# Attention sums and a three-way maxout layer on one core: transposing the normalised k and v sums on VectorE instead of TensorE

## The chip, the cores and the metric

The kernel runs on one NeuronCore of a Trainium2 chip. A core has five engines that run side by side, each with its own queue of instructions in order: TensorE (PE in the profile; its weight loads are shown as PEld), VectorE (DVE), ScalarE (ACT), GpSimd (POOL) and SyncE (SP). TensorE reads SBUF and writes PSUM, which here is eight banks of 2 KB on each of 128 partitions. The metric is the device time of one execution in microseconds (us), as the median of several runs.

## The reference

Two parts in a row. The first one squeezes k and v of each of 8 batches and 8 heads (576 positions, 64 wide) to 32 slots, and lets q attend to the slots; the second one takes the largest of three linear maps of the result, and maps that back:

```
a = exp(phi - max(phi)) ; a = a / sum(a over positions)      # phi: 8, 8, 576, 32
k_m = einsum('bhsm,bhsd->bhmd', a, k) ; v_m = einsum('bhsm,bhsd->bhmd', a, v)
attn = softmax(q @ k_m^T / 8) ; x = attn @ v_m               # per batch and head
x -> (8 * 576, 512)
h = max(x @ w1, x @ w2, x @ w3)                              # w: 512 x 768
out = h @ w_out                                              # 768 x 512
```

## The kernel before

The work goes batch by batch, but the batches overlap. Heads are taken in pairs: NP = 4 pairs, NG = 2 halves, and slots of four pairs fill 128 partitions (M = 32 slots each). The maps w1 and w2 have w3 subtracted once, so that x @ w3 is added only at the end; and the weights are multiplied into the slots of v ("fold"), so that x itself is never formed.

For each batch these steps run; the letter is the one that the order uses for it:

- L0 to L3 load phi, k, v and q through GpSimd's queue (lines 94, 98 and 111), which casts k, v and q to bf16; r0 and r1 pack k and v into one tile kvr on GpSimd (line 104). Tiles of two buffers each are loaded again as soon as their readers are done; a load that waits for them holds up GpSimd's queue behind it.
- E is the exponential of phi on ScalarE (line 258). B sums k, v and ones over the positions with 72 small matmuls into PSUM (line 278).
- N normalises on VectorE: a reciprocal (298), v times it (302), and k times it in two instructions (312). They fill kvn, 128 partitions by three blocks of 128 (v, and k as even and odd columns).
- K transposes the three blocks of kvn, 128 x 128 each, by three matmuls against the identity (line 327) into one PSUM bank, and one copy brings the result to kvt (128 x 384, bf16; line 189 on ScalarE or 193 on VectorE). Batches 0 and 1 do k and v apart, as K0 and K1.
- Q0 and Q1 transpose q on VectorE (342). S multiplies k's part of kvt with q (362), 32 small matmuls, and takes the exponential (371).
- a, s, c, m, X turn the scores to attention for batches 1 to 7: transpose in blocks of 32 (416), sum (424), reciprocal (433) on VectorE, multiply on GpSimd (438), transpose back (446) on VectorE. Batch 0 does it in another way (M, R).
- D0 to D2 and D3 fold v's part of kvt into the weights (matmuls of line 469, evacuated to wp or wp3). D4 and V belong to batch 0 alone.
- F0 to F11 are the hidden layer (495): four matmuls each. The even one is evacuated as h (187 on ScalarE, 191 on VectorE), the odd one is combined with it by a maximum on VectorE (508).
- T0 to T4 are the last layer: six matmuls of line 557 with the hidden values and two of line 542 with the slots (four of line 533 for T4), an evacuation to ot and a store on SyncE's queue. P does three of the six ahead, p the two with the slots.

Nothing is scheduled automatically: a long string at line 652 lists the steps, and each engine executes its share of them in that order. "!" after a step swaps the engine of its evacuation between ScalarE and VectorE, "^" splits the evacuation in two halves, one for each. A second string of digits (line 146) names the PSUM bank of each step that needs one. So a step that stands behind another in the string waits for it on every engine that both use. The part around the change, in the order before:

```
L1@4 a1@2 L2@4 T2@1! s1@2 ... E@3 F2@2 F3@2 L2@5 L1@5 F8@2 F0@2 F9@2 B@3 N@3 D3@2 F1@2
P3@2 Q0@3 L0@5 Q1@3 F4@2 P2@2 K@3! p2@2 F5@2 S@3 ...
```

Of the kernel before, what the change touches and what calls it, by code (L numbers as in the profile page):

```python
# [9 lines left out]
BF16 = mybir.dt.bfloat16  # L10
# [5 lines left out]
def kernel(  # L16
# [12 lines left out]
    nc = tc.nc  # L29

    B, H, S, D = q.shape
    M = phi.shape[-1]
    P = 128
    NP = H // 2
    NG = NP // 2
    HP = P // 2
    NC = S // HP
    R = 32
# [3 lines left out]
    SH = S // 2  # L42
    BANK = 512
    HEAD = 3

    const = ctx.enter_context(tc.tile_pool(name="const", bufs=1))
    inp = ctx.enter_context(tc.tile_pool(name="inp", bufs=2))
    work = ctx.enter_context(tc.tile_pool(name="work", bufs=2))
# [74 lines left out]
    def load_wo():  # L123
        nc.gpsimd.dma_start(out=wo_sb, in_=moe_w_out.rearrange("(t p) c -> p t c", p=P))
# [16 lines left out]
    for i in range(P // M):  # L141
# [4 lines left out]
    banks = iter(  # L146
        "".join(
            """
            60606026024506014014024062406420461246246742404462642602462046246367404603260260
            42062046274240402606206420462406142142646204764260426046206426402762604260420624  # L150
            07042604506421026264124026420402462064206026462467676767
            """.split()
        )
    )
# [1 line left out]
    def one_bank():  # L156
        return psum[:, int(next(banks))]
# [50 lines left out]
    def w3_o_head(j):  # L208
        po = one_bank()
        for f in range(HEAD):  # L210
            nc.tensor.matmul(
# [5 lines left out]
            )  # L217
        w3_heads[j] = po, HEAD

# [28 lines left out]
        )  # L248

    ln = const.tile([P, S], FP32, name="ln")  # L250
    ONES = {(0, 0), (0, 1)}
    st = {}

# [37 lines left out]
    def att_kv_norm(b, part=None):  # L291

        s = st[b]
        kvp = s["kvp", part]
        if part != 1:
            rden = s["rden"] = work.tile([P, NG], FP32, name="rden")
            s["kvn"] = work.tile([P, 3, P], BF16, name="kvn")
            nc.vector.reciprocal(out=rden, in_=kvp[:, :, D if part == 0 else 2 * D])
        rden, kvn = s["rden"], s["kvn"]
        if part != 0:  # L300
            v0 = 0 if part == 1 else D
            nc.vector.tensor_tensor(
                out=kvn[:, 0].rearrange("p (a d) -> p a d", a=NG),
                in0=kvp[:, :, v0 : v0 + D],
                in1=rden.unsqueeze(2).to_broadcast([P, NG, D]),
                op=ALU.mult,
            )
        if part == 1:
            return
        for g in range(NG):  # L310
            kn = kvn[:, 1:3, HP * g : HP * (g + 1)]
            nc.vector.tensor_scalar_mul(
                out=kn.rearrange("p h (t d) -> p h t d", t=2),
                in0=kvp[:, g, 0:D]
                .rearrange("p (d h) -> p h d", h=2)
                .unsqueeze(2)
                .to_broadcast([P, 2, 2, R]),
                scalar1=rden[:, g : g + 1],
            )

    def att_kv_t(b, swap, part=None):

        s = st[b]
        ns = {None: slice(0, 3), 0: slice(1, 3), 1: slice(0, 1)}[part]
        ps = one_bank().bitcast(BF16)[:, 0 : 3 * P].rearrange("p (n m) -> p n m", n=3)
        for n in range(3)[ns]:
            nc.tensor.transpose(ps[:, n], s["kvn"][:, n], ident)  # L327
        if part != 1:
            s["kvt"] = work.tile([P, 3, P], BF16, name="kvt")
        evacuate("K", 0, swap, s["kvt"][:, ns], ps[:, ns])  # L330
        if b == 0 and part != 0:
            s["kvtn"] = const.tile([P, P], BF16, name="kvtn")
            nc.scalar.mul(out=s["kvtn"], in_=ps[:, 0], mul=-1.0)

    def att_q(b, n):


        s = st.setdefault(b, {})
        if "qT" not in s:
            s["qT"] = work.tile([P, NP, NC, R, 2], BF16, name="qT")  # L340
        j = halves[n]
        nc.vector.transpose(  # L342
            out=s["qT"][:, j].rearrange("p j c r e -> p (j c r e)").bitcast(FP32),
            in_=loaded[b]["q"][:, j].rearrange("p j c d -> p (j c d)").bitcast(FP32),
        )
# [270 lines left out]
    def issue(b, n, swap):  # L616

        i = int(n[1:]) if len(n) > 1 else None
        {
            "I": lambda: [make_identity(nc, ident)]  # L620
            + [nc.gpsimd.memset(x[:, :, :, 2 * D : 2 * D + 1], 1.0) for x in kvrs],
            "Y": lambda: load_w(i) if i < 3 else load_wo(),
            "L": lambda: load_ph(b) if i == 0 else load_q(b) if i == 3 else load_kv(b, i - 1),
            "H": lambda: load_kv(b, i % 2, halves[i // 2]),
            "r": lambda: pack(b, i),
            "E": lambda: [att_exp(b, h) for h in (halves if b == 0 else [slice(0, NP)])],
            "B": lambda: att_kv(b, i),
            "N": lambda: att_kv_norm(b, i),
            "K": lambda: att_kv_t(b, swap, i),
            "Q": lambda: att_q(b, i),  # L630
            "S": lambda: att_score(b),
            "a": lambda: att_t(b, i),
            "s": lambda: att_sum(b, i),
            "c": lambda: att_rec(b, i),
            "m": lambda: att_mul(b, i),
            "X": lambda: (ones_mul if (b, i) in ONES else att_back)(b, i),
            "M": lambda: ones_sum(b, i),
            "R": lambda: ones_rec(b, i),
            "D": lambda: fold(b, i, swap),
            "F": lambda: ffn1(b, i, swap),  # L640
            "P": lambda: ffn2_hidden(b, i, range(HEAD)),
            "p": lambda: ffn2_slots(b, i),
            "J": lambda: w3_o_head(i),
            "T": lambda: ffn2(b, i, swap),
            "W": lambda: w3_t(i, swap),
            "O": lambda: w3_o(i, swap),
            "V": lambda: w_diff(i),
            "G": lambda: wait_for(b, i),
            "Z": lambda: warm_up(i),
        }[n[0]]()  # L650


    for w in """
        E@0 H0@0 H2@0 L3@0 Z25@0 B0@0 I@0 N0@0 Z2@0 K0@0! Q0@0 Q1@0 Z9@0 S@0 Z2@0 M0@0 M1@0
        R0@0 Y2@0 G0@0 R1@0 W0@0 Y3@0 W1@0 W2@0 H1@0 H3@0 Y0@0 Z6@0 O0@0! X1@0 X0@0 Y1@0 L0@1
        O1@0 B1@0 N1@0 O3@0! L1@1 K1@0! O2@0! D1@0^ D0@0^ L3@1 D3@0^ V0@0 L2@1 F8@0 F10@0 F2@0!
        V1@0 F0@0 F6@0 L2@2 F4@0! L1@2 D2@0 V2@0 D4@0 p1@0 E@1 F3@0 F1@0 p0@0 F11@0 F5@0 F9@0
        P1@0 F7@0 B0@1 P3@0 N0@1 P0@0 Q1@1 Q0@1 K0@1! L0@2 L3@2 T1@0 L0@3 S@1 T3@0 B1@1 V4@0
        L1@3 p2@0 a0@1 s0@1 N1@1 K1@1! P2@0 c0@1 m0@1 a1@1 s1@1 c1@1 D0@1 D2@1!^ m1@1 X0@1 X1@1
        D1@1!^ T2@0 T0@0! F2@1 F6@1! F8@1 F3@1 F7@1 F0@1 L2@3 F4@1 r1@2 r0@2 F1@1 E@2 F9@1 F5@1  # L660
        F10@1 L3@3 F11@1 L0@4 P2@1 B@2 N@2 Q0@2 D3@1 T0@1! K@2! Q1@2 T1@1 S@2 a0@2 s0@2 c0@2
        L1@4 a1@2 L2@4 T2@1! s1@2 m0@2 c1@2 X0@2 D2@2 m1@2 D0@2! D1@2! X1@2 T4@1 r0@3 T3@1 r1@3
        F6@2 F10@2!^ F7@2 L3@4 F11@2 E@3 F2@2 F3@2 L2@5 L1@5 F8@2 F0@2 F9@2 B@3 N@3 D3@2 F1@2
        P3@2 Q0@3 L0@5 Q1@3 F4@2 P2@2 K@3! p2@2 F5@2 S@3 p3@2 a0@3 a1@3 s0@3 L3@5 c0@3 s1@3
        m0@3 T3@2 D0@3 D2@3!^ E@4 c1@3 X0@3 m1@3 D1@3! T2@2 T0@2! X1@3 r1@4 T1@2! F2@3 F4@3!
        r0@4 F3@3 F0@3!^ L2@6 Q1@4 F6@3 F5@3 F8@3 F7@3 F10@3 B@4 N@4 D3@3 P0@3 Q0@4 F11@3 K@4!
        F9@3 F1@3 p1@3 L1@6 L0@6 P1@3 L3@6 r1@5 D1@4! S@4 a0@4 r0@5 s0@4 c0@4 E@5 T0@3! a1@4
        T3@3 m0@4 s1@4 T1@3 c1@4 X0@4 D2@4!^ B@5 D0@4 N@5 m1@4 D3@4 Q0@5 L1@7 T4@3! X1@4 Q1@5
        K@5! F6@4!^ F8@4!^ S@5 F7@4 F9@4 F10@4 F4@4 F5@4 F0@4 F2@4 a1@5 r1@6 F11@4 L2@7 a0@5
        r0@6 F3@4 E@6 L0@7 F1@4 s0@5 T2@3! D2@5^ c0@5 D0@5 B@6 L3@7 N@6 D1@5! T1@4 s1@5 m0@5  # L670
        Q1@6 c1@5 K@6! Q0@6 m1@5 r1@7 T3@4 X0@5 X1@5 S@6 F2@5!^ a0@6 F10@5!^ F3@5 F8@5 F11@5
        F0@5 s0@6 F6@5 E@7 F4@5^ F1@5 F9@5 F7@5 a1@6 T2@4! F5@5 r0@7 D0@6^ D1@6! B@7 N@7 D3@5!^
        T0@4 Q0@7 c0@6 K@7 T2@5! D2@6!^ s1@6 c1@6 Q1@7 m0@6 D1@7 D3@7 T0@5! P3@5 S@7 a0@7 s0@7
        m1@6 a1@7 X0@6 T3@5 D2@7!^ D3@6 D0@7 X1@6 s1@7 c0@7 T4@5! F4@6 F0@6 F10@6! F8@6!^ F5@6
        c1@7 m0@7 F6@6 m1@7 F1@6 F9@6 T1@5 X1@7 X0@7 F11@6 F2@6 F10@7! F6@7 F2@7 F3@6 F7@6
        F4@7! F0@7 F11@7 T2@6 F3@7 F1@7 F7@7 T0@6 F8@7 F9@7 F5@7 T1@6! T0@7! T4@7! T1@7 T3@6
        T2@7 T3@7
    """.split():
        n, b = w.rstrip("!^").split("@")
        issue(int(b), n, w[len(n) + 1 + len(b) :])  # L680
# [30 lines left out]
```

## Time and profile before

| | before |
|---|---|
| median of 3 runs | 164.09 us (163.59 to 164.92) |
| the profiled execution | 163.59 us |
| its span, first to last instruction | 161.8 us |
| TensorE matmuls busy | 152.2 us, 2058 instructions |
| VectorE busy | 110.1 us, 212 instructions |
| ScalarE busy | 87.5 us, 140 instructions |
| GpSimd busy | 69.6 us, 72 instructions |
| granted TensorE clock | 0.995 of full speed on average |

The busy time of an engine is the time in which at least one of its instructions runs. TensorE's matmuls are pipelined, so that each lasts longer than the distance to the next. The profile also has the chain of waits: it begins at the last instruction and goes back, at each step to what released it, or to the instruction before it on its engine. Groups of instructions have the line of kernel.py that issued them (L327 is line 327), the engine, the operation, what is written and read, shapes as partitions x elements, the count, then busy time in us and the mean of one in ns.

### The profile page before, as it was taken

How to read it: one execution, taken by the hardware profiler on the slowest of the kernel's cores; microseconds unless marked ns; L12 is line 12 of the kernel's file. 1: busy time of each engine (PE TensorE's matmuls, PEld its weight loads, DVE VectorE, ACT ScalarE, POOL GpSimd, SP SyncE). 2: the span in 40 equal slices, each digit the busy share in tenths (PEclk: the TensorE clock that was granted, in tenths of full speed). 3: DMA queues.
4: the chain of work that ended last, by engine and by line, in shares of the span. 5: the costliest groups of instructions: out<-in, count | busy, mean ns of one | idle time of the engine just before them, and what ended most of it. 6: DMA issues, size and time to landing. Idle time of an engine off the chain costs nothing.

```text
span 161.8 us, 4860 instructions
## 1 busy us (share of the span) xinstructions
PE 152.2 (94%) x2058; PEld 86.0 (53%) x2080; DVE 110.1 (68%) x212; ACT 87.5 (54%) x140; POOL 69.6 (43%) x72
## 2 busy tenths in 40 slices
PE   7988799999999999999999999999999999999990
PEld 2343454664476436644764467557543477663460
DVE  2013456999997578879895988979888976774020
ACT  4104414934676595759465987768537955111310
POOL 7266224111599039915958986537204050000000
PEclk9999999999999999999999999999999999999998
DMA  5999999999999999999999999999222311013333
GB/s 151 157 200 205 201 211 209 280 208 210 233 310 296 251 239 283 301 217 208 249 311 245 209 321 282 208 289 274 69 86 95 127 65 65 0 69 124 136 130 132
DMA packets 21974, 31.77 MB, mean 196 GB/s; under 512 B 1216, under 2 KB 16576, under 8 KB 21952
## 3 DMA queue, kind: packets, MB, share of 16 engines
q0 software_dynamic: 16080, 21.43, 69.1%
q1 hardware_dynamic: 5728, 9.90, 17.5%
q8 instruction: 16, 0.26, 0.6%
q10 hardware_dynamic: 144, 0.13, 0.2%
q14 instruction: 6, 0.05, 0.1%
HBM read 39.32 MB, written 9.44 MB: 301 GB/s over the span
## 4 chain that ended last, share of the span: by engine, by line
PE 73%; DMA 14%; DVE 5%; POOL 3%; issue 2%; ACT 1%; POOLq 0%
PE psum L495 28%; PE psum L557 25%; DMA w_sb<-in_moe_w_dram 9%; PE psum L542 7%; PE psum L469 5%; DMA kvo<-in_k_dram 4%; PE psum L278 3%; DVE hT L508 2%; PE psum L362 2%; POOL t L438 1%; POOL kvo L98 1%; PE psum L533 1%; PE psum L593 1%; DVE qT L342 1%; PE psum L327 1%
## 5 line engine op out<-in xcount | busy, mean ns | idle before, releaser
L557 PE MATMUL psum<-wo_sb,hT 128*128 128x512 bf16 x194 | 50.3, 380 | 1.5 <-issue 0.9
L495 PE MATMUL psum<-attn,wp 128*128 128x288 bf16 x384 | 50.6, 286 | 0.1
L495 PEld LDWEIGHTS <-wp 128*128 128x128 bf16 x384 | 37.1, 98 | 13.2 <-issue 0.9
L508 DVE TENSOR_TENSOR hT<-psum,h 128x576 bf16<-128x576 f32 x48 | 34.4, 750 | 6.5 <-PE psum L495 3.8
L187 ACT ACTIVATE h<-psum 128x576 bf16<-128x576 f32 (+1 forms) x41 | 23.6, 609 | 14.1 <-PE psum L495 13.8
L557 PEld LDWEIGHTS <-hT 128*128 128x128 bf16 x210 | 19.0, 98 | 22.8 <-issue 4.6
L438 POOL TENSOR_TENSOR t<-t,sm 128x576 bf16<-128x576 bf16 x14 | 16.2, 1154 | 31.8 <-DVE sm L433 31.7
L189 ACT CAST wp<-psum 128x1024 bf16<-128x1024 f32 (+2 forms) x31 | 24.3, 835 | 7.4 <-PE psum L469 7.2
L104 POOL COPY kvr<-kvo 128x2304 bf16<-128x2304 bf16 x12 | 25.1, 2111 | 5.0 <-DMA kvo<-in_v_dram 2.7
L189 ACT COPY ot<-psum 128x512 f32<-128x512 f32 x26 | 15.2, 592 | 21.1 <-PE psum L542 17.5
L542 PE MATMUL psum<-wp,attn 128*128 128x512 bf16 x59 | 17.8, 379 | 0.3 <-issue 0.3
L167 PE MATMUL psum<-warm 128*128 128x512 bf16 x42 | 12.6, 457 | 1.4 <-DVE warm L136 1.2
L193 DVE COPY ot<-psum 128x512 f32<-128x512 f32 x9 | 6.1, 681 | 10.8 <-PE psum L542 10.8
L342 DVE STREAM_TRANSPOSE qT<-qq 128x576 f32<-128x576 f32 x16 | 11.8, 754 | 1.3 <-DMA qq<-in_q_dram 1.2
L371 ACT ACTIVATE e<-psum 128x576 bf16<-128x576 f32 x16 | 9.6, 651 | 4.0 <-PE psum L362 3.8
L258 ACT ACTIVATE e<-ph 128x1152 bf16<-128x1152 f32 (+1 forms) x9 | 9.6, 1061 | 2.8 <-DMA ph<-in_phi_dram 2.7
L189 ACT COPY kvt<-psum 128x384 bf16<-128x384 bf16 (+2 forms) x9 | 3.7, 410 | 13.3 <-PE psum L327 13.2
L191 DVE TENSOR_SCALAR h<-psum 128x288 bf16<-128x288 f32 (+1 forms) x15 | 8.7, 590 | 2.9 <-PE psum L495 2.9
L193 DVE CAST wp<-psum 128x512 bf16<-128x512 f32 (+2 forms) x14 | 10.1, 731 | 0.8 <-PE psum L469 0.7
L424 DVE TENSOR_REDUCE sm<-t 128x18 f32<-128x576 bf16 x14 | 10.3, 739 | 0.2
L416 DVE STREAM_TRANSPOSE t<-e 128x288 f32<-128x288 f32 x14 | 6.5, 462 | 5.8 <-ACT e L371 5.7
L111 POOL DMA_DIRECT2D qq<-in_q_dram x8 | 6.0, 756 | 9.2 <-DVE h L191 3.3
(60 smaller groups left out, 130.1 us busy)
## 6 DMA issues: line engine op xcount, KB each, us to landing
out_dram<-ot SPq DMA_DIRECT2D x35, 256.0 KB, 5.5
qq<-in_q_dram POOLq DMA_DIRECT2D x8, 576.0 KB, 16.9
ph<-in_phi_dram POOLq DMA_DIRECT2D x7, 576.0 KB, 18.7
kvo<-in_k_dram POOLq DMA_DIRECT2D x7, 576.0 KB, 19.7
kvo<-in_v_dram POOLq DMA_DIRECT2D x7, 576.0 KB, 17.1
w_sb<-in_moe_w_dram POOLq DMA_DIRECT2D x3, 768.0 KB, 14.7
wo_sb<-in_moe_w_out_dram POOLq DMA_DIRECT2D x1, 768.0 KB, 10.3
ph<-in_phi_dram SPq DMA_DIRECT2D x2, 288.0 KB, 3.2
```

The lines of the kernel that those rows point to most:

```text
L104: nc.gpsimd.tensor_copy(out=kvrs[b % 2][:, :, :, D * i : D * (i + 1)], in_=kvos[b % 2][:, 1 - i])
L167: nc.tensor.matmul(po[:, 0:BANK], lhsT=warm[:, 0:P], rhs=warm, start=True, stop=True)
L187: nc.scalar.activation(out=out_, in_=in_, func=AF.Relu)
L189: nc.scalar.copy(out=out_, in_=in_)
L193: nc.vector.tensor_copy(out=out_, in_=in_)
L342: nc.vector.transpose(out=s["qT"][:, j].rearrange("p j c r e -> p (j c r e)").bitcast(FP32), in_=loaded[b]["q"][:, j].rearrange("p j c d - ...
L424: nc.vector.tensor_reduce(out=sm, in_=s["t", g].rearrange("p n r e -> p n e r"), op=ALU.add, axis=mybir.AxisListType.X,)
L438: nc.gpsimd.tensor_tensor(out=t, in0=t, in1=s["sm", g].unsqueeze(2).to_broadcast([P, S // HP, R, 2]), op=ALU.mult,)
L495: nc.tensor.matmul(acc[:, h, 0:SH], lhsT=wps[b][:, g, w * DF + ft * P : w * DF + (ft + 1) * P], rhs=attn[:, g, c0 : c0 + SH], start=(g == ...
L508: nc.vector.tensor_tensor(out=hT[:, ft, (b % 2) * S : (b % 2 + 1) * S].rearrange("p (h n) -> p h n", h=2), in0=a, in1=s["h1", ft], op=ALU.max,
L542: nc.tensor.matmul(po, lhsT=attn[:, g, c0 : c0 + P], rhs=wp3s[b][:, g, :], start=(g == 0 and not done), stop=(last and g == NG - 1),)
L557: nc.tensor.matmul(po, lhsT=hT[:, fc, c0 : c0 + P], rhs=wo_sb[:, fc, :], start=(n == ns[0] and not done), stop=(last and n == ns[-1]),)
```

## The change

For batches 2 to 7, K is replaced by k. N writes kvn in another arrangement of columns: four groups of 96, each with 32 columns of v and of the two halves of k. Then VectorE transposes the whole kvn at once (128 x 384), in blocks of 32 x 32, into a new tile kvm. Sixteen copies put the 32-partition pieces of kvm in their places in kvt: four groups of columns times four groups of partitions, those with odd j on ScalarE, the others on GpSimd, 32 partitions x 96 elements each, to other partitions than they come from. TensorE and PSUM take no part in it. Batches 0 and 1 keep K0 and K1. The whole order is new, and with it the string of banks and the marks for the evacuations; among others, the load of phi for batch 1 comes behind that of its k, and the parts of T that are done ahead differ: P2@1 is gone, and p3@1, p1@1, p3@4 and P1@6 are new.

```diff
+    MOVED = range(2, B)
...
+    kvm = const.tile([P, P // R, 3, R], BF16, name="kvm")
...
+        if b in MOVED:
+            kb = kvn.rearrange("p n m -> p (n m)").rearrange("p (x n d) -> p x n d", x=P // R, n=3)
+            vn = kb[:, :, 0].rearrange("p (a h) d -> p a h d", a=NG)
+            kns = [kb[:, 2 * g : 2 * g + 2, 1:3].rearrange("p t h d -> p h t d") for g in range(NG)]
+        else:
+            vn = kvn[:, 0].rearrange("p (a h d) -> p a h d", a=NG, h=2)
+            kns = [
+                kvn[:, 1:3, HP * g : HP * (g + 1)].rearrange("p h (t d) -> p h t d", t=2)
+                for g in range(NG)
+            ]
...
+    def att_kv_move(b):
+
+        s = st[b]
+        nc.vector.transpose(
+            out=kvm.rearrange("p x n m -> p (x n m)"),
+            in_=s["kvn"].rearrange("p n m -> p (n m)"),
+        )
+        kvt = s["kvt"] = work.tile([P, 3, P], BF16, name="kvt")
+        for x in range(P // R):
+            for j in range(NP):
+                r = slice(M * j, M * (j + 1))
+                move = nc.scalar.copy if j % 2 else nc.gpsimd.tensor_copy
+                move(out=kvt[R * x : R * (x + 1), :, r], in_=kvm[r, x])
...
+            "k": lambda: att_kv_move(b),
...
+        R0@0 Y2@0 G0@0 R1@0 W0@0 Y3@0 W1@0 W2@0 H1@0 H3@0 Y0@0 Z6@0 O0@0! X1@0 X0@0 Y1@0 O1@0
+        L1@1 B1@0 N1@0 L0@1 O2@0! L3@1 K1@0! L2@1 O3@0! D1@0^ D0@0^ D3@0^ F10@0 F8@0 V0@0 F4@0!
+        V1@0 F0@0 F6@0 L2@2 F2@0! D2@0 V2@0 D4@0 L1@2 p1@0 L0@2 F3@0 F1@0 F11@0 p0@0 F5@0 F7@0
+        P0@0 E@1 F9@0 B0@1 N0@1 P3@0 L3@2 P1@0 K0@1! Q1@1 T1@0 Q0@1 V4@0 S@1 a0@1 s0@1 T3@0
+        B1@1 p2@0 N1@1 c0@1 L2@3 m0@1 a1@1 s1@1 c1@1 K1@1! X0@1 P2@0 D0@1 D2@1 D1@1!^ m1@1 L0@3
+        X1@1 r1@2 T0@0! T2@0 F2@1^ L1@3 F6@1! r0@2 F4@1 F0@1 F7@1 F10@1 E@2 L3@3 F5@1 F1@1 L1@4
+        F11@1 F3@1 F8@1 F9@1 B@2 D3@1 L2@4 N@2 L0@4 k@2 T0@1 p3@1 Q0@2 Q1@2 p1@1 T2@1! S@2 a0@2
+        s0@2 a1@2 c0@2 r1@3 T3@1 T1@1 m0@2 s1@2 c1@2 D2@2^ m1@2 X0@2 D1@2! D0@2^ T4@1! X1@2
+        F10@2 r0@3 F11@2 E@3 F2@2!^ F3@2 F0@2 F1@2 L3@4 F4@2 L2@5 B@3 D3@2 F6@2 N@3 k@3 Q0@3
+        F5@2 L1@5 F8@2 p2@2 F7@2 Q1@3 P3@2 P2@2 F9@2 p3@2 S@3 a0@3 T3@2 s0@3 T0@2! r0@4 T2@2!
+        a1@3 c0@3 s1@3 c1@3 L0@5 D0@3 m0@3 X0@3 m1@3 D1@3! X1@3 D2@3 T1@2! F0@3!^ F6@3!^ F1@3
+        E@4 F2@3 Q1@4 L3@5 L1@6 F7@3 F10@3 r1@4 L2@6 B@4 N@4 D3@3 F4@3 Q0@4 F8@3 k@4 F11@3 F9@3
+        F3@3 P1@3 F5@3 P0@3 p1@3 D2@4 S@4 a0@4 T1@3 T0@3! r1@5 E@5 a1@4 s0@4 s1@4 c1@4 L0@6
+        T3@3 r0@5 D1@4^ D3@4 B@5 c0@4 L3@6 m1@4 N@5 X1@4 m0@4 D0@4 k@5 Q0@5 X0@4 T4@3 Q1@5 T2@3
+        F0@4!^ r0@6 L1@7 F10@4!^ S@5 F11@4 F1@4 F2@4 a0@5 s0@5 F4@4 F8@4 F3@4 r1@6 F9@4 F6@4
...
+        D0@5 D2@5 T1@4 X1@5 Q1@6 F4@5! F0@5!^ F6@5!^ F8@5 F10@5 k@6 Q0@6 F11@5 F2@5! F1@5 F9@5
+        T2@4 S@6 a0@6 F3@5 r0@7 F5@5 F7@5 E@7 T0@4 D1@6^ r1@7 D3@5 B@7 N@7 D3@6 a1@6 k@7 Q1@7
+        Q0@7 s1@6 c1@6 P3@5 T1@5! m1@6 T2@5! s0@6 S@7 T3@5 a0@7 s0@7 D1@7! c0@6 D2@6!^ a1@7
```

More of the change, by code (lines that the diff above doesn't have):

```diff
@@ L148 @@
             """
-            60606026024506014014024062406420461246246742404462642602462046246367404603260260
-            42062046274240402606206420462406142142646204764260426046206426402762604260420624
-            07042604506421026264124026420402462064206026462467676767
+            60606026024506014014024062406420462146246742404462462042602460246745206025024062
+            46024602126424261426420642064206126460426106240624064206404602462402406246024604
+            62045026206506246024604206402604260246024110101012
             """.split()
@@ L302, in att_kv_norm @@
             nc.vector.tensor_tensor(
-                out=kvn[:, 0].rearrange("p (a d) -> p a d", a=NG),
-                in0=kvp[:, :, v0 : v0 + D],
-                in1=rden.unsqueeze(2).to_broadcast([P, NG, D]),
+                out=vn,
+                in0=kvp[:, :, v0 : v0 + D].rearrange("p a (h d) -> p a h d", h=2),
+                in1=rden.unsqueeze(2).unsqueeze(3).to_broadcast([P, NG, 2, R]),
                 op=ALU.mult,
@@ L310, in att_kv_norm @@
         for g in range(NG):
-            kn = kvn[:, 1:3, HP * g : HP * (g + 1)]
             nc.vector.tensor_scalar_mul(
-                out=kn.rearrange("p h (t d) -> p h t d", t=2),
+                out=kns[g],
                 in0=kvp[:, g, 0:D]
@@ L654 @@
         E@0 H0@0 H2@0 L3@0 Z25@0 B0@0 I@0 N0@0 Z2@0 K0@0! Q0@0 Q1@0 Z9@0 S@0 Z2@0 M0@0 M1@0
[L655 to L677, printed above, removed]
+        R0@0 Y2@0 G0@0 R1@0 W0@0 Y3@0 W1@0 W2@0 H1@0 H3@0 Y0@0 Z6@0 O0@0! X1@0 X0@0 Y1@0 O1@0
@@ new lines @@
+        T3@3 r0@5 D1@4^ D3@4 B@5 c0@4 L3@6 m1@4 N@5 X1@4 m0@4 D0@4 k@5 Q0@5 X0@4 T4@3 Q1@5 T2@3
+        F0@4!^ r0@6 L1@7 F10@4!^ S@5 F11@4 F1@4 F2@4 a0@5 s0@5 F4@4 F8@4 F3@4 r1@6 F9@4 F6@4
+        c0@5 F5@4 F7@4 p3@4 L2@7 a1@5 s1@5 m0@5 E@6 c1@5 m1@5 L0@7 L3@7 T3@4 D1@5^ B@6 X0@5 N@6
+        D0@5 D2@5 T1@4 X1@5 Q1@6 F4@5! F0@5!^ F6@5!^ F8@5 F10@5 k@6 Q0@6 F11@5 F2@5! F1@5 F9@5
+        T2@4 S@6 a0@6 F3@5 r0@7 F5@5 F7@5 E@7 T0@4 D1@6^ r1@7 D3@5 B@7 N@7 D3@6 a1@6 k@7 Q1@7
+        Q0@7 s1@6 c1@6 P3@5 T1@5! m1@6 T2@5! s0@6 S@7 T3@5 a0@7 s0@7 D1@7! c0@6 D2@6!^ a1@7
@@ L678 @@
+        D0@6^ m0@6 X1@6 T0@5 D3@7 s1@7 c0@7 c1@7 D0@7 m0@7 X0@6 D2@7 m1@7 X0@7 T4@5! F6@6 F0@6^
+        X1@7 F7@6 F2@6 F1@6 F10@6 F8@6! F11@6 F0@7 F3@6 F9@6 F10@7 F1@7 F11@7 F4@6!^ F2@7! F4@7
+        F6@7 F8@7 F5@7 F7@7 F9@7 P1@6 F5@6 F3@7 T3@6 T1@6 T4@7 T1@7! T0@6 T2@6 T0@7 T2@7 T3@7
     """.split():
```

## The prediction

> **What bounds the kernel now.** I read the chain of waits in order of time first, then the busy times, then stretches of the middle, then the single forms of instructions. The chain ends like this (start, length, what):
>
> ```profile
> 44.52 0.02 issue
> 44.55 0.49 DVE attn L446
> 45.04 0.04 issue
> 45.08 5.79 PE psum L495 x46
> ...
> 53.88 0.43 PE psum L542 x2
> 54.31 0.17 PE psum L327 x3
> 54.48 1.29 PE psum L557 x6
> ...
> 157.93 0.23 PE psum L601 x2
> 158.16 0.02 issue
> 158.19 0.37 ACT ot L613
> ```
>
> Behind 45.08 us every piece up to 158.16 is TensorE work or a few hundredths of "issue". I added those "issue" pieces up from the whole chain: 1.5 us of 113.1 us. So TensorE alone sets the time there, and work taken off it is worth its own length, as long as nothing else comes late. The three transposes of a batch (L327) stand on the chain with 0.17 us, six times for batches 2 to 7 (at 54.31, 70.02, 84.31, 94.41, 106.01 and 119.29 us). Before 45 us the chain is on the loads of the weights up to 26.4 us, then mostly on VectorE from 31.8 to 45 us; batches 0 and 1 are at work there.
>
> The stretch from 44 to 148 us, cut into seven, sums to this (busy us):
>
> ```profile
> 90.00:106.00 16.00, 15.65 (x306) 9.53 (x307) 14.34 (x32) 13.22 (x22) 11.01 (x10) 1.00 1.17 255
> ...
> sum 104.00, PE 102.44 PEld 60.93 DVE 83.72 ACT 66.75 POOL 52.55; mean PE 14.63 PEld 8.70 DVE 11.96 ACT 9.54 POOL 7.51
> ```
>
> The columns are TensorE's matmuls, its weight loads, VectorE, ScalarE and GpSimd; the granted clock is 1.00. VectorE is the next engine, 80% busy, and 90% in the fullest stretch. The forms that price the change (busy us, mean ns behind the count):
>
> ```profile
> L104 POOL COPY kvr<-kvo 128x2304 bf16<-128x2304 bf16 x12 | 25.1, 2111 | 5.0 <-DMA kvo<-in_v_dram 2.7 <-DMA kvo<-in_k_dram 2.3
> ...
> L342 DVE STREAM_TRANSPOSE qT<-qq 128x576 f32<-128x576 f32 x16 | 11.8, 754 | 1.3 <-DMA qq<-in_q_dram 1.2
> ...
> L258 ACT ACTIVATE e<-ph 128x1152 bf16<-128x1152 f32 x7 | 8.2, 1170 | 0.5 <-DMA ph<-in_phi_dram 0.5
> ...
> L416 DVE STREAM_TRANSPOSE t<-e 128x288 f32<-128x288 f32 x14 | 6.5, 462 | 5.8 <-ACT e L371 5.7
> ...
> L401 ACT ACTIVATE r<-ln 128x576 f32<-128x576 f32 x2 | 1.4, 682 | 0.1
> ...
> L621 POOL MEMSET kvr<- 128x36 bf16 x2 | 0.4, 298 | 0.0
> ...
> L131 POOL COPY gate<-kvo 1x2 bf16<-1x2 bf16 x1 | 0.2, 175 | 4.3 <-DMA kvo<-in_k_dram 4.3
> ```
>
> **What is removed.** 18 TensorE transposes: six pieces of 0.17 us on the chain, 1.02 us. Each is issued 57 ns after the one before; the 219 ns that a row gives for one is its pipelined length. Five ScalarE copies of kvt (482 ns) and one of VectorE (296 ns) go too; they are off the chain.
>
> The Trainium skill's page "TensorE: Matmul & The Clock Gate" (Part 4: PE-mode transpose) gives about 275 ns for one such transpose inside a kernel; 18 of them would be 4.95 us, so the end would come near 159.1 us. The chain's 0.17 us for three speaks against it.
>
> **What is added.** A transpose of 384 bf16 elements on VectorE for each of six batches. From the two forms above, (754 - 462) / 288 = 1.01 ns an element, so 462 + 96 x 1.01 = 0.56 us. If a bf16 element went at half that, it would be 0.37 us; I take 0.56, since both rows stream one element at a time. Then 16 copies of 32 partitions x 96 elements, eight on ScalarE, eight on GpSimd. No row has 32 partitions or a shift of partitions. ScalarE: slope (1170 - 682) / 576 = 0.85 ns, so 682 - 480 x 0.85 = 275 ns. Two exponentials of 651 ns in a row took 1.19 us in the timeline, so neighbours overlap by 0.11 us, and eight take 8 x 0.275 - 7 x 0.11 = 1.43 us (2.2 without overlap). GpSimd: from 1x2 to 2304 elements the slope is 0.84 ns, so 175 + 94 x 0.84 = 254 ns; two packs in a row took 4.15 us for 2 x 2.11, an overlap of 0.07, so eight take 1.54 us. Bounds: 175 ns each (0.9 us for eight) if the fixed part were all, and 400 ns each (3.2 us) if writes in short runs are slow, as the 298 ns for a memset of only 36 scattered elements hints. I take 254, nearest to the packs, which write runs of 64.
>
> **What is moved between engines.** Counting the marks of both orders, six evacuations of ot go from ScalarE to VectorE (679 against 593 ns), two whole and one half of wp leave VectorE (1184 and 673 ns), and a little of h is split. VectorE: 6 x 0.56 - 0.30 + 6 x 0.68 - 3.04 + 0.90 = +5.0 us, to 89 of 104 us. ScalarE: 48 x 0.275 - 5 x 0.482 + 3.07 - 0.60 - 0.47 - 6 x 0.593 = +9.2, to 76. GpSimd: 48 x 0.254 = +12.2, to 65. None reaches TensorE's 102, so no engine becomes the bound by its sum.
>
> **The new wait.** S (or D) of a batch now waits for copies on two engines. From the end of the kv matmuls to the end of the norm was 1.07 us in batch 5 (matmuls to 103.95, VectorE from 104.01 to 105.02). Then 0.56 for the transpose, 0.05 to hand over, 1.54 for GpSimd's copies and 0.14 until TensorE starts (kvt written by 95.40, S from 95.54): 3.36 us with empty queues. TensorE's cover, by the new order with pieces from the chain (F 0.49, T 1.72, P 0.65, p 0.43, D 0.23, T4 1.84): batch 2: D3 T0 p3 p1 T2, 4.53 us; batch 3: D3, five F, two p, two P, 4.84; batch 4 (up to D2): D3, six F, P1, P0, p1, 4.90; batch 5: D0 T4 T2 F0 F10, 4.77; batch 6: two D, T1, nine F, T2, 8.31; batch 7: D3 P3 T1 T2, 4.32. On VectorE's queue ahead of the transpose stand Q0 in batch 4 (0.75), c0 and X1 in batch 5 (0.71), 3.3 us in batch 6, a1 in batch 7 (0.46). On GpSimd's queue ahead of the copies are two load issues in batch 2 (2 x 0.75, done while VectorE works 1.63), and in batch 5 a load and two multiplies (3.06 us, of which B hides 0.67: 2.39, equal to VectorE's 2.35). Margins: 1.2, 1.5, 0.8, 0.7, 1.6 and 0.5 us. Behind the waiting copies stand GpSimd's packs and loads of the next batches; by the page's last part those loads land 17 to 20 us after their issue, queued behind others, so a delay of 1.5 us at the issue is covered. What can eat a margin is one hT step of VectorE (0.75 us) still queued when the norm comes: then batch 7 is 0.25 late. I put in 0.2 us for this. Loads: batch 1's phi goes behind its k in the queue, some 3 us later; its exponential is also later in the order, so it is hidden; without cover 3 us at most.
>
> **The sum.** Profiled run: 163.59 us (span 161.8) - 1.02 + 0.2 = 162.8. The median of the runs is 0.5 higher, so 163.3 us.
>
> **Rivals.** Slower: copies on GpSimd longer than I take. With x us beyond 1.54 for eight, batches are late by x less their margin. At 400 ns each (x = 1.66) this gives 0.46 + 0.16 + 0.86 + 0.96 + 0.06 + 1.16 = 3.7 us, so 164.09 - 1.02 + 3.7 = 166.8 us. It decides for slower by over 1% from about 375 ns a copy. For it: the scattered memset, no row with 32 partitions; VectorE's +5 us works the same way. Against: the packs' 0.84 ns an element. 0.24. Faster than my sum: the new order also closes TensorE's gaps, at most the 1.5 us of "issue", so 161.6 to 162.4. For it: the order is new throughout; against: most gaps are hundredths where the kind of matmul changes, and those stay. 0.12. Transposes at 275 ns: 159.1, 0.03. The change doing nothing measurable, all gain eaten by late starts of S: 164.1, inside my own case.
>
> **How the numbers follow.** My case, 162.6 to 164.6, gets 0.61. About 1%, 1.64 us, is what a measurement of this kernel can tell from no change: faster is below 162.45, slower above 165.73. Faster takes the gaps, the dear transposes and the low edge of my case: 0.17. Slower takes the dearer part of its rival, above 375 ns, 0.22. The rest, 0.61, is the same. The range, 162.0 to 166.2, leaves out the dear transposes, the deepest closing of gaps and copies above some 385 ns.
>
> **What would show it.** L327 falls from 24 to 6; the chain stays on TensorE from 45 us; VectorE's new transpose near 0.56 us, copies near 0.25 on GpSimd and 0.28 on ScalarE; TensorE's idle time before L362 and L469 stays under 0.5 us. I am wrong if idle time before L362 is put down to kvt on GpSimd or ScalarE in several batches, or if the chain goes through VectorE after 45 us.

## The result: 0.6% faster, with the copies of one batch late

| | before | changed |
|---|---|---|
| median of 14 runs each | 163.85 us | 162.94 us (162.44 to 163.50) |
| ratio to before | | 0.9944 (95%: 0.9924 to 0.9964) |
| span of the profiled execution | 161.8 us | 161.0 us |
| F2 of batch 1 to the last matmul, by the chain | 113.08 us | 112.10 us |
| VectorE, ScalarE, GpSimd busy | 110.1, 87.5, 69.6 us | 113.9, 97.0, 81.9 us |

The row of the chain is the one used below for single effects: the stretch from the first matmul of F2 of batch 1 that the chain has (the third, 45.08 us before, 45.25 now) to the end of TensorE's work. What lies ahead of it follows the loads and ended anywhere between 44.8 and 46.3 us in the executions of these kernels, so spans are not compared to tenths. The stretch is 0.98 us shorter, and its start came 0.17 us later. One execution of the last kernel below, the profiled one, took 537 us where the others took 163; it is left out of that ratio, and gives no stretch.

The first part of the changed kernel's page, busy time of each engine:

```profile
PE 152.3 (95%) x2062; PEld 84.9 (53%) x2062; DVE 113.9 (71%) x222; ACT 97.0 (60%) x179; POOL 81.9 (51%) x120
```

The same chain of waits as before the change, in order of time, for the changed kernel:

```profile
45.25 5.79 PE psum L520 x46
51.04 0.73 PE psum L280 x68
51.77 0.23 PE psum L494 x8
52.00 1.40 PE psum L582 x6
53.40 1.29 PE psum L567 x6
54.70 1.29 PE psum L582 x6
55.99 0.43 PE psum L567 x2
56.42 0.41 PE psum L387 x24
...
122.66 0.61 PE psum L387 x25
...
157.12 0.23 PE psum L626 x2
```

Lines have moved: F is L520, the last layer L582, L567 and L558, the fold L494, the sums of k and v L280, S is L387. No transpose of batches 2 to 7 is left on the chain, and TensorE still carries it alone from 45 us. S of batch 2 stands there with 0.41 us, that of batch 7 with 0.61: there alone TensorE waited, 0.2 us.

The sums over the middle, from 44 to 148 us as before, with the same columns:

```profile
90.00:106.00 16.00, 16.00 (x305) 9.39 (x304) 15.12 (x34) 13.31 (x25) 14.00 (x19) 1.00 1.15 259
...
sum 104.00, PE 103.78 PEld 60.17 DVE 85.31 ACT 78.41 POOL 65.81; mean PE 14.83 PEld 8.60 DVE 12.19 ACT 11.20 POOL 9.40
```

VectorE is at 85, ScalarE at 78, GpSimd at 66 of 104 us; in the fullest stretch GpSimd went from 11.0 to 14.0 of 16. TensorE's 103.8 against 102.4 before is not more work: the trace of before lacks some matmul records (194 matmuls beside 210 weight loads for the last layer, here 210 beside 210), and where one is missing the chain shows "issue". The rows and a piece of the chain, before:

```profile
L557 PE MATMUL psum<-wo_sb,hT 128*128 128x512 bf16 x194 | 50.3, 380 | 1.5 <-issue 0.9
...
L557 PEld LDWEIGHTS <-hT 128*128 128x128 bf16 x210 | 19.0, 98 | 22.8 <-issue 4.6
...
52.48 0.16 issue
52.64 1.24 PE psum L557 x5
```

Those 0.16 and 1.24 us for five matmuls are together the 1.40 us that six take at 52.00 in the changed kernel.

The forms of the new instructions:

```profile
L344 ACT COPY kvt<-kvm 32x96 bf16<-32x96 bf16 x48 | 12.9, 269 | 2.0 <-DVE kvm L335 1.2
L344 POOL COPY kvt<-kvm 32x96 bf16<-32x96 bf16 x48 | 12.4, 259 | 13.9 <-DVE kvm L335 6.7 <-PE psum L520 4.9
...
L335 DVE STREAM_TRANSPOSE kvm<-kvn 128x384 bf16<-128x384 bf16 x6 | 3.3, 555 | 0.1
...
L352 PE MATMUL psum<-ident,kvn 128*128 128x128 bf16 x6 | 1.0, 222 | 0.4 <-DVE kvn L323 0.4
```

One copy lasts 259 or 269 ns, the transpose 555 ns. What eight of them take is in the timeline (start, length, engine, line); batch 2 first:

```profile
53.07 0.58 DVE L335 STREAM_TRANSPOSE kvm<-kvn 128x384 bf16<-128x384 bf16 x1
...
53.68 2.28 ACT L344 COPY kvt<-kvm 32x96 bf16<-32x96 bf16 x8 [0.63 <-DVE kvm L335]
53.71 2.43 POOL L344 COPY kvt<-kvm 32x96 bf16<-32x96 bf16 x8 [0.47 <-DVE kvm L335]
...
119.64 0.54 DVE L335 STREAM_TRANSPOSE kvm<-kvn 128x384 bf16<-128x384 bf16 x1
...
120.33 2.44 POOL L344 COPY kvt<-kvm 32x96 bf16<-32x96 bf16 x8 [3.87 <-DVE kvm L335]
...
122.59 0.39 PEld L387 LDWEIGHTS <-kvt 32*32 32x32 bf16 x32 [0.42 <-POOL kvt L344]
```

Eight copies take GpSimd 2.43 us and ScalarE 2.28: one starts every 0.31 or 0.285 us, more than the length of one, so neighbours do not overlap at all. In batch 2 the copies end at 56.14, and S starts with no gap at 56.42. In batch 7 (from 119.64 on) they end at 122.77; TensorE was through with the last layer at 122.66, and S, which takes its pieces of kvt as they come, is drawn out by 0.2 us.

### The profile page after: what moved, and what is told of

Read it like the earlier page. It is cut to its first block, busy times and chain, and to the rows that moved or that the text cites. A ratio compares the mean times of both kernels' runs of the same rounds, so it can differ in the third digit from the quotient of the medians.

```text
span 161.0 us, 4938 instructions
## 1 busy us (share of the span) xinstructions
PE 152.3 (95%) x2062; PEld 84.9 (53%) x2062; DVE 113.9 (71%) x222; ACT 97.0 (60%) x179; POOL 81.9 (51%) x120
## 3 DMA queue, kind: packets, MB, share of 16 engines
q0 software_dynamic: 16080, 21.43, 69.6%
## 4 chain that ended last, share of the span: by engine, by line
PE 77%; DMA 14%; POOL 4%; DVE 2%; issue 1%; ACT 0%; POOLq 0%
PE psum L520 30%; PE psum L582 27%; DMA w_sb<-in_moe_w_dram 9%; PE psum L567 8%; PE psum L494 5%; DMA kvo<-in_k_dram 4%; PE psum L280 3%; PE psum L387 2%; POOL kvo L99 2%; PE psum L558 1%; POOL t L463 1%; DVE qT L367 1%; PE psum L618 1%; POOL wo_sb L125 0%; DVE hT L533 0%
## 5 line engine op out<-in xcount | busy, mean ns | idle before, releaser
L582 PE MATMUL psum<-wo_sb,hT 128*128 128x512 bf16 x210 | 51.3, 380 | 0.0
L520 PE MATMUL psum<-attn,wp 128*128 128x288 bf16 x384 | 50.2, 286 | 0.2 <-DVE attn L471 0.2
L520 PEld LDWEIGHTS <-wp 128*128 128x128 bf16 x384 | 37.1, 98 | 13.3 <-issue 1.3
L533 DVE TENSOR_TENSOR hT<-psum,h 128x576 bf16<-128x576 f32 x48 | 33.8, 746 | 4.9 <-PE psum L520 2.4
L582 PEld LDWEIGHTS <-hT 128*128 128x128 bf16 x210 | 19.1, 98 | 24.0 <-issue 4.8
L190 ACT CAST wp<-psum 128x1024 bf16<-128x1024 f32 (+2 forms) x33 | 26.4, 860 | 6.5 <-PE psum L494 6.5
L344 POOL COPY kvt<-kvm 32x96 bf16<-32x96 bf16 x48 | 12.4, 259 | 13.9 <-DVE kvm L335 6.7
L567 PE MATMUL psum<-wp,attn 128*128 128x512 bf16 x62 | 18.1, 379 | 0.0
L194 DVE COPY ot<-psum 128x512 f32<-128x512 f32 x15 | 10.2, 677 | 9.9 <-PE psum L567 5.8
L190 ACT COPY ot<-psum 128x512 f32<-128x512 f32 x20 | 11.7, 592 | 8.6 <-PE psum L567 6.0
L99 POOL DMA_DIRECT2D kvo<-in_v_dram x9 | 6.6, 739 | 16.5 <-PE psum L280 13.1
L344 ACT COPY kvt<-kvm 32x96 bf16<-32x96 bf16 x48 | 12.9, 269 | 2.0 <-DVE kvm L335 1.2
L168 PE MATMUL psum<-warm 128*128 128x512 bf16 x44 | 11.8, 421 | 1.2 <-DVE warm L137 1.2
L192 DVE TENSOR_SCALAR h<-psum 128x288 bf16<-128x288 f32 (+1 forms) x17 | 9.4, 575 | 0.8 <-ACT ot L190 0.4
```

What stands on the lines that cost most here:

```text
L168: nc.tensor.matmul(po[:, 0:BANK], lhsT=warm[:, 0:P], rhs=warm, start=True, stop=True)
L190: nc.scalar.copy(out=out_, in_=in_)
L344: move(out=kvt[R * x : R * (x + 1), :, r], in_=kvm[r, x])
L520: nc.tensor.matmul(acc[:, h, 0:SH], lhsT=wps[b][:, g, w * DF + ft * P : w * DF + (ft + 1) * P], rhs=attn[:, g, c0 : c0 + SH], start=(g == ...
L533: nc.vector.tensor_tensor(out=hT[:, ft, (b % 2) * S : (b % 2 + 1) * S].rearrange("p (h n) -> p h n", h=2), in0=a, in1=s["h1", ft], op=ALU.max,
L567: nc.tensor.matmul(po, lhsT=attn[:, g, c0 : c0 + P], rhs=wp3s[b][:, g, :], start=(g == 0 and not done), stop=(last and g == NG - 1),)
```

## The experiments

Ratios are to the kernel before, measured beside each on its chip, with 95% intervals. "The stretch" is the one of the table. Theory A, where the expectations use letters, is that the gain is the length of the 18 transposes on TensorE, less the late start of batch 7, and that the new order gains nothing by itself. Rival B is that the new order and the shifted evacuations bring the gain. In diffs, steps of the order are shown without the rest of their line.

### What a transpose costs on TensorE

Before, with each of the 18 transposes issued four times:

```diff
-        for n in range(3)[ns]:
-            nc.tensor.transpose(ps[:, n], s["kvn"][:, n], ident)
+        for _ in range(4 if part is None else 1):
+            for n in range(3)[ns]:
+                nc.tensor.transpose(ps[:, n], s["kvn"][:, n], ident)
```

> The kernel before with each of the 18 transposes of batches 2 to 7 issued four times into the same place: 54 more. At 57 ns each, as the chain has it: 3.1 us more, 166.9 us, ratio 1.019. At 275 ns each: 14.9 us more, 178.7 us. If TensorE were not the bound there: no change.

Measured: 166.29 against 163.95 us, 1.0140 (1.0114 to 1.0166), less than the 3.1 us expected. 54 more transposes cost 2.3 us, 43 ns each (35 to 50 by the interval); the stretch of the profiled execution, 115.86 us, grew by 2.78, 51 ns each. Its chain has six pieces of this kind:

```profile
54.04 0.67 PE psum L328 x12
```

0.67 us for twelve is 56 ns each; before, three had 0.17. So 18 transposes are worth 0.8 to 1.0 us, and not the 4.95 us of the rival with 275 ns each. This trace of the old order has all 210 matmuls of the last layer, and no "issue" in the stretch.

### The new order with the transposes on TensorE

The order and marks of the changed kernel, k taken out, and K put in some steps later in front of S. Where to put K, and in which PSUM bank, is a choice; I made it twice. First:

```diff
-    MOVED = range(2, B)
+    MOVED = range(0)
...
- N@2 L0@4 k@2 T0@1 p3@1
+ N@2 L0@4 T0@1 K@2! p3@1
...
- F8@2 p2@2
+ F8@2 K@3! p2@2
...
- k@4 F11@3 F9@3
+ F11@3 K@4! F9@3
```

(and K@5! behind T4@3, K@6! behind T1@4, K@7! behind T1@5).

> The new order, marks and loads, but batches 2 to 7 transposed on TensorE again (three transposes and one ScalarE copy, put 1.7 to 2.6 us of TensorE work behind the sums, so that nothing waits). Theory A, the gain is the length of 18 transposes at 57 ns and the new order gains nothing by itself: 1.0 us above the changed kernel, that is the time of before within 0.3 us, ratio 0.998 to 1.003. Rival B, the new order and the moved evacuations bring the gain: the time of the changed kernel, ratio 0.994. If the order costs something by itself (the first matmul of F2@1 starts 0.17 us later in the changed kernel): ratio 1.001 to 1.003.

Measured: 164.95 against 163.95, 1.0057 (1.0034 to 1.0079), the stretch 113.77. Neither theory had this. The chain shows why, in batch 3:

```profile
69.21 0.65 ACT h L188
69.86 0.38 ACT kvt L190
70.24 0.04 issue
70.28 1.46 PE psum L582 x6
```

TensorE waits, for some 0.2 us, until ScalarE has emptied a hidden layer's bank and then kvt: the next step of the last layer reads neither, so what it waits for is the bank of K, which it was given. In batch 4 the transposes themselves wait 0.6 us for ScalarE's evacuation of a hidden layer. That is a fault of my placing, so this run decides nothing between A and B. The second placing gives K banks that are free by then:

```diff
- F8@2 K@3! p2@2 F7@2 Q1@3 P3@2 P2@2
+ F8@2 p2@2 F7@2 Q1@3 P3@2 K@3! P2@2
...
- F11@3 K@4! F9@3 F3@3 P1@3 F5@3 P0@3
+ F11@3 F9@3 F3@3 P1@3 F5@3 K@4! P0@3
```

> As the first experiment (the new order, TensorE's transposes back in batches 2 to 7), but the transposes of batches 3 and 4 stand 1.6 to 2.1 us later and use a bank that has been free for over 1.5 us; in the first one TensorE waited for ScalarE to free the bank, about 1.4 us on the chain in these two batches. Theory A, the gain is TensorE's length alone: 1.0 us above the changed kernel, ratio to before 0.999 to 1.002. If the transposes cost more than their length in a full order (a bank and an evacuation must be found for each batch): it stays near 1.005. If the order brings the gain: 0.994.

Measured: 164.01 against 163.91, 1.0003 (0.9979 to 1.0026). The six pieces are back, all as this one:

```profile
54.55 0.17 PE psum L352 x3
```

So the order, its marks and its loads are worth nothing that the times resolve (-0.34 to +0.43 us), and rival B's 0.994 is outside. The step from this kernel to the changed one, 1.0003 to 0.9944, is 0.97 us. One thing is left open: in the profiled execution the stretch was 112.79, 0.29 us shorter than before, and began 0.88 us later; the two may belong together, and the times don't tell.

### The new transposes in the old order

The other way round: the old order and marks, k right behind N, K taken out.

```diff
- B@2 N@2 Q0@2 D3@1 T0@1! K@2! Q1@2
+ B@2 N@2 k@2 Q0@2 D3@1 T0@1! Q1@2
```

(the same for batches 3 to 7).

> The old order with its marks, VectorE's transpose and the 16 copies right behind the norm of batches 2 to 7. Theory A with the wait: norm 1.07, transpose 0.56, eight GpSimd copies 2.43 as measured in the changed kernel, hand-overs 0.19, sum 4.25 us; the old order leaves 3.67, 3.43, 3.43, 3.28, 3.67 and 3.90 us of TensorE work between, so the batches are late by 0.58 + 0.82 + 0.82 + 0.97 + 0.58 + 0.35 = 4.1 us, less 1.0 saved: 3.1 us slower than before, about 167 us, with TensorE idle before L387 put down to kvt. If the wait is covered without a new order: 162.9 us.

Measured: 190.08 against 163.95, 1.1612 (1.1568 to 1.1656), a large miss. The list of TensorE's waits (us in all, times, longest) begins so:

```profile
PE psum L520 <- ACT wp L190: 6.4, 2, 3.6
PE psum L567 <- ACT wp L190: 6.3, 3, 3.2
PE psum L582 <- ACT wp L190: 3.0, 1, 3.0
```

It does not wait for kvt, the tile that the copies write, but for ScalarE's evacuation of wp, the folded weights. L567, the slots' matmuls of the last layer, read these weights (6.3 us). L582 does not read them, and L520 reads some that had been folded before, so these 9.4 us must be waits for the PSUM bank that ScalarE empties. The timeline of batch 3:

```profile
73.84 2.23 ACT L344 COPY kvt<-kvm 32x96 bf16<-32x96 bf16 x8 [2.19 <-DVE kvm L335]
...
76.10 1.01 ACT L190 CAST wp<-psum 128x1024 bf16<-128x1024 f32 x1
...
77.16 1.01 PE L567 MATMUL psum<-wp,attn 128*128 128x512 bf16 x2 [2.42 <-ACT wp L190]
```

ScalarE stood 2.19 us at its first copy until VectorE had the transpose, then copied for 2.23 us, and only then evacuated D3 of batch 2, which in this string stands behind k. TensorE waited 2.42 us for it. In the changed kernel the folds near it (D3, in batch 6 D0 and D2) stand ahead of k. The six waits above make 15.7 us. The rest is the granted clock, 0.954 over the whole span against 0.995 before: 186.0 x 0.041 = 7.6 us as an estimate; together 23.3 of the 24.2 us by which the span grew. TensorE's busy time fits: 121.5 us from 44 us on, where the changed kernel has 113.1. One window in the columns used above, TensorE's busy time first, the clock (0.73) behind GpSimd's:

```profile
54.00:60.00 6.00, 2.90 (x7) 0.98 (x7) 1.11 (x2) 3.53 (x10) 3.31 (x10) 0.73 1.21 209
```

To tell the queue from mere lateness, the same order was run with the transpose behind N, and the copies as a step g of their own in K's old place:

```diff
+            "g": lambda: att_kv_place(b),
...
- B@2 N@2 k@2 Q0@2 D3@1 T0@1! Q1@2
+ B@2 N@2 k@2 Q0@2 D3@1 T0@1! g@2 Q1@2
```

> The old order with VectorE's transpose right behind the norm, but the 16 copies where the old order had TensorE's transposes, so that ScalarE's evacuations before that place do not queue behind the copies' wait. If the queueing on ScalarE made the second experiment so slow (the evacuations of wp waited behind the copies, TensorE for their banks, and its clock fell to a half behind each pause): most of the 26 us comes back. Lateness alone then: 2.57 us from the first copy to TensorE, against 1.72, 0.92, 2.06, 0.98, 1.72 and 1.95 us of work left in the old order, late by 0.85 + 1.65 + 0.5 + 1.6 + 0.85 + 0.6 = 6.1 us, less 1.0: 5 us slower than before, 169 us, ratio 1.03. If the lateness itself was the cause: 185 us or more again.

Measured: 173.60 against 164.34, 1.0560 (1.0526 to 1.0595). 17 of the 26 us come back and the clock is at 0.999, so most of that loss was copies that wait at the head of a queue; that it was ScalarE's is read from the waits, since this edit moves GpSimd's copies too. 9.2 us remain, more than the 5 that I expected. The top of TensorE's waits is now attn, with 2.0 us in all, and no wait for a wp of ScalarE is left in the list:

```profile
PE psum L523 <- DVE attn L474: 2.0, 2, 1.3
```

Its chain goes through the copies in batches 2 to 6, and through VectorE and GpSimd between them. This run doesn't say which late step began each of those waits.

### How well the copies are hidden

Twice the work where it matters: the changed kernel with two more copies on GpSimd in each batch, those of x = 3 issued again.

```diff
                 move(out=kvt[R * x : R * (x + 1), :, r], in_=kvm[r, x])
+                if x == P // R - 1 and j % 2 == 0:
+                    move(out=kvt[R * x : R * (x + 1), :, r], in_=kvm[r, x])
```

> The changed kernel with two of GpSimd's eight copies of each batch issued twice: 0.6 us more before kvt is whole. From the changed kernel's profile, the time between the last copy plus 0.14 and the first matmul that reads kvt: 0.14, 0.47, 0.12, 0.2, 0.9 and 0 us in batches 2 to 7. If the copies stand that close to TensorE's path: late by 0.46 + 0.13 + 0.48 + 0.4 + 0 + 0.6 = 2.1 us, 165.0 us, ratio 1.007 to before. If there is more cover than that: 162.9 us.

Measured: 165.57 against 163.95, 1.0110 (1.0069 to 1.0150), that is 2.7 us over the changed kernel. The chain leaves TensorE and goes through the copies in batches 2, 3, 4 and 7, and through GpSimd's loads and packs behind them:

```profile
71.32 0.24 POOL kvt L346
71.56 0.74 POOL kvo L99
72.34 2.10 POOL kvr L105
```

So 0.6 us more on GpSimd in a batch is already past the cover. In batches 3 and 4 the chain does not go on to S: the packs of the next batches come late, and the sums with them.

Half the work: eight of the sixteen copies left out in each batch (j = 2 and 3), kvt in two fixed tiles, so that half of kvt is not renewed in batches 2 to 7.

```diff
-        kvt = s["kvt"] = work.tile([P, 3, P], BF16, name="kvt")
+        kvt = s["kvt"] = kvts[b % 2]
...
+                if j >= 2:
+                    continue
```

> The changed kernel with half of the copies left out (those with j = 2 and 3, so that half of kvt is not renewed in batches 2 to 7): four copies on each engine, 1.2 us less until kvt is whole. Theory A, the copies are hidden but for batch 7: 0.2 us faster, 162.7, ratio 0.993. If the copies also cost time elsewhere, by keeping GpSimd and ScalarE from other work: 0.5 us or more faster, 0.991 or less.

Measured: 162.82 against 163.91, 0.9930 (0.9905 to 0.9956); the stretch 111.92, 0.18 us shorter than with all copies, and S of batch 7 stands with 0.41 us on the chain as in the other batches. In the changed kernel the copies are hidden, then, but for these 0.2 us; the times, 0.9930 beside 0.9944, agree but do not resolve it.

### Two attempts to make it faster

The load L2 of batch 3 stands ahead of batch 1's multiplies on GpSimd's queue, and the chain at the start of the stretch passes through it. Moved behind them:

```diff
- c0@1 L2@3 m0@1 a1@1
+ c0@1 m0@1 a1@1
...
- m1@1 L0@3
+ m1@1 L2@3 L0@3
```

> The changed kernel with the load of v for batch 3 moved behind the two multiplies of batch 1 on GpSimd's queue. In the changed kernel this load waited for the sums of batch 1 and held up the first multiply (42.40 us instead of 41.94 before), and F2@1 began 0.17 us later than before. If that is on the path: 0.2 us faster than the changed kernel, ratio to before 0.993. If not: the same, 0.9944. If the later load makes batch 3 late: slower.

Measured: 163.61 against 163.91, 0.9971 (0.9947 to 0.9995): no gain on the changed kernel, 0.9944; the intervals overlap, so that a loss is not shown either. The chain:

```profile
45.26 0.81 POOL kvo L99
46.07 0.75 POOL ph L95
46.82 2.12 POOL kvr L105
...
49.61 2.12 POOL kvr L105
51.73 0.04 issue
51.77 0.80 PE psum L280 x68
```

The load has not gone; it stands now ahead of the packs of batch 2, and the sums (L280) wait for these. All of this execution is 0.8 us later here than that of the changed kernel, so I count from VectorE's first reciprocal of the scores (L458, at 42.40 us here and 41.60 there). The first multiply begins 0.34 us behind it instead of 0.80, and the last transpose of attn, for which F2 waits, 0.17 us sooner. But the second pack begins 0.59 us later, and the sums only 0.07 us sooner. What the early place of the load costs the multiplies, it spares the packs.

Batch 7's late S: k put directly behind N, ahead of D3 of batch 6 (with the load's move still in).

```diff
- N@7 D3@6 a1@6 k@7
+ N@7 k@7 D3@6 a1@6
```

> As the run before, and VectorE's transpose of batch 7 ahead of a1 of batch 6 (0.47 us earlier). In the changed kernel S of batch 7 began 0.2 us late, on GpSimd's last copy. Theory A: 0.2 us more, 0.4 us faster than the changed kernel, ratio 0.992. If other work was late there too: no change.

Measured: 166.64 against 163.91, 1.0131 (1.0086 to 1.0176), 3.0 us over the run above by the medians and 2.6 by the ratios. It is the trap of the old order once more, in one batch (timeline):

```profile
120.61 2.23 ACT L344 COPY kvt<-kvm 32x96 bf16<-32x96 bf16 x8 [1.12 <-DVE kvm L335]
...
122.86 1.01 ACT L190 CAST wp<-psum 128x1024 bf16<-128x1024 f32 x1
...
123.92 2.04 PE L582 MATMUL psum<-wo_sb,hT 128*128 128x512 bf16 x6 [2.43 <-ACT wp L190]
```

The step back: k ahead of a1 only, D3 still first, and the load where the changed kernel has it.

```diff
- N@7 D3@6 a1@6 k@7
+ N@7 D3@6 k@7 a1@6
```

> The changed kernel with k of batch 7 ahead of a1 of batch 6, but still behind D3 of batch 6, so that ScalarE evacuates wp before it waits for the copies. If the loss of the seventh run came from that evacuation: none of it is left, and S of batch 7 can start 0.2 us earlier, ratio to before 0.993. If it came from a1 being later on VectorE: slower than the changed kernel again, above 1.0.

Measured: 162.98 against 164.34, 0.9907 (0.9880 to 0.9933), the stretch 111.91. The chain passes from the last layer into S of batch 7 with no wait:

```profile
123.46 0.43 PE psum L387 x24
```

To compare it with the changed kernel, both were run again side by side, the changed one first:

> The changed kernel itself, once more, on the same chip as the next run, so that the two are read against the same runs of before: ratio 0.9944 within its interval, 0.992 to 0.997.

> The run before last once more, beside the changed kernel on one chip. If starting S of batch 7 0.2 us earlier is worth its length: 0.2 us faster than the changed kernel, a ratio to it of 0.9985. If the 0.9907 of the first look was the chip: the same as the changed kernel.

Measured: 162.97 against 163.78, 0.9960 (0.9935 to 0.9986), the stretch 112.08, for the changed kernel; 162.96, 0.9946 (0.9926 to 0.9966) for the one with k@7 ahead of a1. The quotient, 0.9986, is the 0.2 us of theory A, but the intervals overlap: the times do not resolve it. That 0.2 us are won rests on the stretch alone, 112.10 and 112.08 in two profiled executions against 111.91 in one, and on S of batch 7 in it, 0.43 against 0.61 us.

## Why the prediction was right, point by point

- **TensorE bounds, and work taken off it is worth its length.** Right. The six pieces of 0.17 us, 1.02 us, went from the chain. The fourfold transposes priced one at 43 to 56 ns, and putting them back on TensorE in the new order cost 0.97 us by the times, or 0.7 against the second measurement of the changed kernel (0.9960).
- **0.2 us for batch 7.** Right in place and size, 0.61 against 0.41 us for S; but not by the hT step of VectorE that I had in mind. The margin was gone because the copies took 0.9 us longer than the sum had them (the next point), and a1 stood ahead of k on VectorE. That the size came out is luck: with these copies my own margins would have given 0.7 us (the point after the next).
- **Eight copies.** The step that was mis-sized. Single copies came out at 259 and 269 ns, where I had 254 and 275. But I took an overlap of neighbours from two long rows, the packs and the exponentials, and gave eight copies 1.54 and 1.43 us. They took 2.43 and 2.28: here there is no overlap but a gap, 0.31 x 7 + 0.26 = 2.43. It was inside the bound of 3.2 that I kept for GpSimd, and over that of 2.2 for ScalarE.
- **The margins.** With 0.9 us taken off, my 1.2, 1.5, 0.8, 0.7, 1.6 and 0.5 become 0.3, 0.6, -0.1, -0.2, 0.7 and -0.4. That is 0.1 + 0.2 + 0.4 us late in batches 4, 5 and 7. Measured, from the copies' end plus the 0.14 us of the hand-over to S (or D) on TensorE, are 0.14, 0.47, 0.12, 0.2 and 0.9 us, and nothing in batch 7. My sums were 0.2 to 0.4 us too strict in batches 4, 5 and 7, so only batch 7 was late, and by less. That the cover is this thin is shown by two more copies: 0.6 us more in a batch, 2.7 us lost.
- **Engine sums.** VectorE +5.0, ScalarE +9.2 and GpSimd +12.2 us were forecast, +3.8, +9.5 and +12.3 measured. None became the bound.
- **The slower rival**, dear copies, turned on 375 ns a copy. In effect each cost 0.31 us, so it stood nearer than my forecast of 254 ns with overlap made it look.
- **The rival that the order closes gaps.** It had nothing to win: the 1.5 us of "issue" before were for the most part missing matmul records, not idle time. So the gaps were not, as I wrote, changes of the kind of matmul. I should have compared matmuls and weight loads of one line, 194 and 210, before counting them.
- **The sum.** 162.8 us for the profiled execution and 163.3 for the median were forecast, 162.81 and 162.94 measured; the half microsecond between the two came from only three runs. Of the 0.98 us by which the stretch shrank, 1.02 - 0.2 = 0.8 is accounted for; the other 0.16 is not. Two executions can differ by as much: the run with fourfold transposes, its six pieces taken back to 0.17 us, has the old order at 112.86 us instead of 113.08.
- **What the prediction did not see** is what the order is for. I costed the copies' wait for those who read kvt, and wrote of GpSimd's loads and packs queued behind them, but nothing of ScalarE's evacuations. In this order they stand ahead of the copies; in the old one they did not, and the same edit cost 26 us.

## What to carry to other kernels

When work moves from the bounding engine to helpers, price it by what one helper instruction costs from start to start in a row of its own kind, not by its length less an overlap seen on larger ones. Then ask at each wait that is added in an in-order queue not only who needs its result, but what else stands behind it: here PSUM evacuations behind a waiting copy stopped TensorE, though nobody yet needed the copy. Before idle time of the bounding engine is counted as something to win, make sure that its records are complete.

## What the chip showed that I had not expected

A short pause of TensorE costs more than itself. In the kernel with k ahead of D3 in batch 7 it paused 2.43 us, to 123.92. Windows of 2 us, with TensorE's busy time first and the granted clock behind GpSimd's:

```profile
121.00:123.00 2.00, 0.49 (x3) 0.10 (x1) 1.97 (x4) 1.91 (x8) 1.65 (x7) 1.00 0.00 0
123.00:125.00 2.00, 1.08 (x5) 0.48 (x5) 1.38 (x3) 0.87 (x1) 1.34 (x2) 0.91 0.20 76
125.00:127.00 2.00, 2.00 (x32) 0.56 (x35) 0.00 (x0) 0.15 (x1) 0.00 (x0) 0.50 0.15 55
127.00:129.00 2.00, 1.67 (x44) 0.59 (x21) 0.73 (x2) 1.63 (x3) 0.00 (x0) 0.73 0.34 128
129.00:131.00 2.00, 2.00 (x31) 0.77 (x23) 2.00 (x5) 1.97 (x4) 1.15 (x1) 1.00 0.28 103
```

The clock fell to 0.50 after the pause and was back at 1.00 some 5 us behind it. The kernel with copies in the old order shows the same, 0.50 from 58 to 60 us after a pause of 3.23 us; the one with late copies, whose longest such wait in the stretch was 1.3 us, stayed at 0.999 on average. The Trainium skill's page "TensorE: Matmul & The Clock Gate" (Why this matters for your kernels) advises against pauses of over about 3 us, since one idle window brings the half clock back; the half clock agrees, but 2.43 us were enough here.

Small copies between SBUF tiles, 32 partitions x 96 elements, start every 0.31 us on GpSimd and every 0.285 us on ScalarE, 50 and 16 ns more than one lasts.
